# A fused sigmoid attention and ReGLU kernel: first keys in two pieces, values lagging four passes, and three blocks transposed by DMA from ScalarE's queue instead of by TensorE

## Chip, cores, metric

One core of one Trainium2 chip. The metric is the device time in microseconds (us), median of several executions. The span of a trace, from the first to the last instruction, is about 2 us shorter than the time of the same execution.

## The reference

```python
# q, k, v: (8, 12, 448, 64)   w_gate, w_val: (768, 1536)   w_out: (1536, 768), float32
attn = sigmoid(q @ k.T / sqrt(64) - log(448)) @ v            # per batch and head, no softmax
x    = attn.transpose(0, 2, 1, 3).reshape(8 * 448, 12 * 64)
out  = (maximum(x @ w_gate, 0) * (x @ w_val)) @ w_out        # (3584, 768)
```

## The kernel before

The 12 heads of each of the 8 batches are worked in three *blocks* of four heads, 24 blocks in all, numbered 0 to 23; blocks 0 to 2 are batch 0, blocks 3 to 5 are batch 1. A block takes 7 *passes*: in each, `scores` multiplies one 64-wide chunk of keys with all queries and ScalarE takes the sigmoid; `values` multiplies the result with v. Batch 0's attention runs alone; after that the passes of the next batch are put between the feed-forward matmuls of the batch at hand, two or three at a time (a *visit*).

The scores' matmuls read q and k transposed, with the 64 features of a head on the partitions. Before, blocks 0 to 5 are transposed by TensorE, 14 small matmuls for each, and copied out of PSUM by VectorE (a part of block 0's by ScalarE). Blocks 6 to 23 are transposed by the DMA engines, on SP's queue.

```python
def dma_transposes(n):                      # blocks 6 to 23
    for nm in ("k", "q"):
        h16 = qk16.pop((nm, n))
        t2 = qkTp.tile([P, NCH, 2, KC], FP16, tag="qkT", name=f"{nm}T")
        nc.sync.dma_start_transpose(
            t2[:].rearrange("p c h k -> p c (h k)"), h16[:].rearrange("p c r d -> p (c r d)"))
        qkT[nm, n] = t2

def transposes(n, nm, *engines):            # blocks 0 to 5
    ...
    for c in range(NCH):
        nc.tensor.transpose(tr[:, c], h16[:, c, :, :], ident[:])
    ...                                     # copies PSUM -> SBUF

def feed(i):                                # after each pass i of batches 1 to 7
    n, c = divmod(i, NCH)
    ...
    m = n + 1
    if c == 4 and NPRO <= m < NB:           # NPRO = 6
        dma_transposes(m)
    if c == 5 and NBLK < m < NPRO:          # blocks 4 and 5
        transposes(m, "k"); transposes(m, "q")

order = halves("g", 0) + halves("u", 0) + [3] + halves("g", 1) + halves("u", 1)
order += [4] + halves("g", 2) + halves("u", 2) + halves("o", 0) + [5]
order += halves("o", 1) + halves("o", 2)    # weight pieces, and the inputs of blocks 3, 4, 5
...
for b in range(B):
    ...
    for step, cost in enumerate(ffn(b)):
        if b == 0 and step == 12:
            transposes(NBLK, "k"); transposes(NBLK, "q")        # block 3
        if order and step % 8 == 0:
            start_next()                    # load and cast the next of `order`
        if todo and t >= todo[0]:
            todo.pop(0); visit()
```

All weights (18 pieces of 768 KB) are loaded by SP, in one queue, and so are the block inputs but for three of the first (k and v of block 0, k of block 2, on ScalarE's queue). Staging buffers (`sw`, five of them, and `st`, ten) hold what has landed until GpSimd has cast it to fp16.

## Time and profile before

| | |
|---|---|
| time | 434.59 us, median of 3 (434.58 to 435.0) |
| TensorE busy | 97% of the span |
| first feed-forward matmul | 28.25 us |
| DMA engines | full from 2 to 66 us, 380 to 390 GB/s |
| last piece of w_out usable | 67.4 us, 2.7 us before TensorE needs it |

The kernel is a stream of matmuls without gaps once the first attention phase is over, and up to 66 us the DMA engines are just as full. The lines behind this table are in the prediction.

The profiled execution of the kernel before is one of 437.15 us with a span of 434.6: the granted clock of TensorE (the share of its full clock that the profile shows) was 0.50 from 27.8 to 31.2 us. Most other executions have spans of 432.4 to 433.1 at a mean clock of 0.995 to 1.000.

### The profile page before, as it was taken

The numbers are of one execution on the slowest core, as the hardware profiler recorded it, in microseconds if no ns is written. First come the engines' busy times: TensorE is split into PE (matmuls) and PEld (weight loads), VectorE is DVE, ScalarE is ACT, GpSimd is POOL, SyncE is SP. The second block draws the span as 40 slices with busy tenths as digits, with TensorE's granted clock in tenths as the row PEclk, the third lists the DMA queues.
The fourth block names the chain that finished last, engine by engine and source line by source line (L and its number), as shares of the span: only waits on it lengthen the run. The fifth ranks groups of instructions, "written<-read, shape, count | busy, mean of one in ns | idle before, by whom it ended". The sixth has DMA issues, their size and how long they took to land.

```text
span 434.6 us, 7877 instructions
## 1 busy us (share of the span) xinstructions
PE 421.6 (97%) x3292; PEld 216.9 (50%) x3292; DVE 102.8 (24%) x172; ACT 235.6 (54%) x325; POOL 100.6 (23%) x130
## 2 busy tenths in 40 slices
PE   7779999999999999999999999999999999999996
PEld 5334554544455445544455454554455444455553
DVE  3632331123201322113211232023220232212210
ACT  5955656655566555555546556565555556532221
POOL 0287758213301313113031133023130100000000
PEclk9989999999999999999999999999999999999999
DMA  8999999791228910596216932199114320030014
GB/s 306 385 384 386 391 391 271 221 265 72 42 74 231 301 37 16 144 262 170 42 38 193 255 128 44 42 242 293 21 24 109 80 44 2 14 96 1 2 36 110
DMA packets 64100, 66.98 MB, mean 154 GB/s; under 512 B 35776, under 2 KB 54336, under 8 KB 64064
## 3 DMA queue, kind: packets, MB, share of 16 engines
q1 hardware_dynamic: 63088, 64.89, 51.2%
q10 hardware_dynamic: 976, 1.57, 1.0%
q8 instruction: 26, 0.43, 0.4%
q14 instruction: 10, 0.08, 0.1%
HBM read 47.19 MB, written 11.01 MB: 134 GB/s over the span
## 4 chain that ended last, share of the span: by engine, by line
PE 95%; ACT 4%; issue 1%; POOL 0%; DVE 0%; ACTq 0%; POOLq 0%
PE gv_ps L225 51%; PE y_ps L251 26%; PE qk_ps L172 9%; PE pv_ps L196 7%; ACT PT L182 3%; PE tr L157 1%; PE fill L336 1%; ACT gate_sb L237 0%; ACT kT L162 0%; POOL ident masks.py:199 0%; DVE ysb L269 0%; ACT ysb L268 0%; POOL ident masks.py:197 0%; POOL bias_t L63 0%; ACTq L182 0%
## 5 line engine op out<-in xcount | busy, mean ns | idle before, releaser
L182 ACT ACTIVATE PT<-qk_ps,bias_t 128x896 f16<-128x896 f32 x168 | 158.1, 1006 | 55.9 <-PE qk_ps L172 55.7
L225 PE MATMUL gv_ps<-xT,wg 128*128 128x448 f16 x576 | 128.5, 355 | 0.0
L225 PE MATMUL gv_ps<-xT,wv 128*128 128x448 f16 x576 | 128.3, 354 | 0.0
L251 PE MATMUL y_ps<-wo,hT 128*128 128x512 f16 (+1 forms) x672 | 114.1, 326 | 0.0
L237 ACT ACTIVATE gate_sb<-gv_ps 128x448 f32<-128x448 f32 x96 | 52.3, 544 | 93.5 <-PE gv_ps L225 93.5
L240 DVE TENSOR_TENSOR hT<-gate_sb,gv_ps 128x448 f16<-128x448 f32 x96 | 59.6, 621 | 168.7 <-PE gv_ps L225 135.8
L251 PEld LDWEIGHTS <-hT 128*128 128x128 f16 x672 | 64.0, 98 | 48.1 <-issue 7.5
L225 PEld LDWEIGHTS <-wv 128*128 128x128 f16 x576 | 54.8, 98 | 57.1 <-issue 9.1
L225 PEld LDWEIGHTS <-wg 128*128 128x128 f16 x576 | 55.0, 98 | 54.6 <-issue 7.1
L209 DVE TENSOR_SCALAR xT<-pv_ps 128x448 f16<-128x448 f32 x48 | 27.7, 620 | 133.1 <-PE pv_ps L196 133.0
L172 PE MATMUL qk_ps<-qT,kT 64*64 64x448 f16 x672 | 51.6, 360 | 6.6 <-ACT PT L182 6.0
L116 POOL CAST v<-st_v 128x448 f16<-128x448 f32 x21 | 11.8, 562 | 173.2 <-PE pv_ps L196 172.6
L273 ACT ACTIVATE ysb<-y_ps 128x512 f32<-128x512 f32 (+1 forms) x55 | 27.1, 493 | 40.6 <-PE y_ps L251 40.3
L196 PE MATMUL pv_ps<-PT,v 64*64 64x448 f16 x672 | 40.2, 351 | 1.3 <-ACT PT L182 0.8
L172 PEld LDWEIGHTS <-kT 64*64 64x64 f16 x672 | 15.8, 105 | 37.3 <-issue 33.0
L109 POOL CAST h16q<-st_q 128x896 f16<-128x896 f32 x21 | 19.6, 932 | 33.3 <-DMA kT<-h16k 32.5
L196 PEld LDWEIGHTS <-v 64*64 64x64 f16 x672 | 20.1, 107 | 13.5 <-issue 1.8
L109 POOL CAST h16k<-st_k 128x896 f16<-128x896 f32 x21 | 19.6, 932 | 1.3 <-DMA qT<-h16q 0.8
L141 POOL CAST wg<-st_wg 128x1536 f16<-128x1536 f32 x6 | 8.9, 1484 | 18.1 <-DMA st_wg<-in_moe_w_gate_dram 18.1
L117 POOL CAST v<-st_v 64x448 f16<-64x448 f32 x21 | 11.7, 559 | 1.3
L118 POOL CAST v<-st_v 64x448 f16<-64x448 f32 x21 | 11.7, 557 | 0.9
L141 POOL CAST wo<-st_wo 128x1536 f16<-128x1536 f32 x6 | 8.8, 1468 | 6.2 <-DMA st_wo<-in_moe_w_out_dram 6.2
(28 smaller groups left out, 51.6 us busy)
## 6 DMA issues: line engine op xcount, KB each, us to landing
st_q<-in_q_dram SPq DMA_DIRECT2D x24, 448.0 KB, 4.7
out_dram<-ysb SPq DMA_DIRECT2D x54, 192.0 KB, 2.7
st_v<-in_v_dram SPq DMA_DIRECT2D x23, 448.0 KB, 5.9
st_k<-in_k_dram SPq DMA_DIRECT2D x22, 448.0 KB, 5.2
st_wg<-in_moe_w_gate_dram SPq DMA_DIRECT2D x6, 768.0 KB, 11.9
st_wu<-in_moe_w_val_dram SPq DMA_DIRECT2D x6, 768.0 KB, 12.2
st_wo<-in_moe_w_out_dram SPq DMA_DIRECT2D x6, 768.0 KB, 11.9
st_k<-in_k_dram ACTq DMA_DIRECT2D x2, 448.0 KB, 6.6
```

What stands on the lines that cost most here:

```text
L109: eng.tensor_copy(o, i)
L116: eng.tensor_copy(t[:, 0], st[:, 0])
L141: eng.tensor_copy(dst, st[:])
L172: nc.tensor.matmul(ps[o : o + 64, bank, 0:S], kT[r : r + 64, c, h, :], qT[r : r + 64, :, h, :], start=True, stop=True, tile_position=(r, o ...
L182: nc.scalar.activation(pt[:], ps[:, :, 0:S], AF.Sigmoid, bias=bias_t[:], scale=qk_scale)
L196: nc.tensor.matmul(pv[pr][o : o + 64, 0:S], t[r : r + 64, pr, c * D : (c + 1) * D], pt[r : r + 64, pr, :], start=(c == 0), stop=(c == NCH ...
L209: nc.vector.tensor_scalar(out=x[:], in0=pv[pr][:, 0:S], scalar1=XSCALE, scalar2=None, op0=AOP.mult)
L225: nc.tensor.matmul(acc[:, 0:S], w[:, dc, jj * P : (jj + 1) * P], xT[b, dc][:], start=(dc == 0), stop=(dc == NDC - 1),)
L237: nc.scalar.activation(g_sb[:], acc[:, 0:S], AF.Relu)
L240: nc.vector.tensor_tensor(out=hT[f][:, o : o + S], in0=g_sb[:], in1=ps[1][:, 0:S], op=AOP.mult)
L251: nc.tensor.matmul(y[:, 0:mn], hT[f][:, o : o + P], wo[f // FG][:, f % FG, m0 : m0 + mn], start=(f == 0), stop=(f == NFC - 1),)
L273: nc.scalar.activation(ysb[:, m0 : m0 + mn], y[:, 0:mn], AF.Copy, scale=OUT_SCALE)
```

## The change

Three things are meant. The start is to be earlier: K of block 0 comes in two pieces, the fillers (matmuls that nobody reads, issued while the first loads are under way) are wider, v is cast by GpSimd, and values lag four passes instead of two. TensorE is to be relieved of the transposes of blocks 3, 4 and 5, which go to DMA; since SP's queue is full of weights, they are issued from ScalarE's queue, and block 6's pair with them, one visit later than before. Batch 0 gets 11 visits instead of 10. And the last output block is copied out of two PSUM banks side by side. The core of the diff:

```diff
-        load_block(0, ("q", q, nc.sync), ("k", k, nc.scalar), ("v", v, nc.scalar))
+        load_block(0, ("q", q, 0, NCH, sp), ("k", k, 0, 4, act), ("k2", k, 4, NCH, sp), ("v", v, 0, NCH, act))
 ...
-            nc.sync.dma_start_transpose(
+            (nc.scalar if n <= NPRO else nc.sync).dma_start_transpose(
 ...
-        if c == 4 and NPRO <= m < NB:
+        if c >= (5 if m <= NPRO else 4) and m not in transposed and NBLK < m < NB:
+            transposed.add(m)
             dma_transposes(m)
-        if c == 5 and NBLK < m < NPRO:
-            transposes(m, "k")
-            transposes(m, "q")
 ...
-        i1 = min(i0 + (3 if c == 0 else 2), NPASS)
+        i1 = min(i0 + (3 if c == 0 and n > NBLK else 2), i0 + NCH - c, NPASS)
 ...
-            if i >= LAG:                                    # LAG = 2
-                m, cm = divmod(i - LAG, NCH)
-                values(m, [cm])
+            while done <= i - (4 if i < NP0 - 4 else 2):
+                values(done // NCH, [done % NCH])
+                done += 1
 ...
-                count = 3 * NBLK + (1 if b == 0 else 0)
-                lo = 4.0 if b == 0 else 0.0
+                count = 3 * NBLK + (2 if b == 0 else 0)
+                lo = 6.0 if b == 0 else 0.0
 ...
-                if b == 0 and step == 12:
-                    transposes(NBLK, "k")
-                    transposes(NBLK, "q")
+                if b == 0 and step == 4:
+                    dma_transposes(NBLK)
```

More of the change, by code (lines that the diff above doesn't have):

```diff
@@ L86, in load_block, with cast_qk @@
         b, i = divmod(n, NBLK)
-        for nm, src, eng in which:
+        for nm, src, c0, c1, eng in which:
             st = stp.tile([P, 2, S], FP32, tag="st", name=f"st_{nm}")
-            eng.dma_start(
-                st[:],
-                src[b, i * HB : (i + 1) * HB].rearrange("(r h) (p c) d -> (h p) r (c d)", h=2, c=NCH),
-            )
+            rows = src[b, i * HB : (i + 1) * HB].rearrange("(r h) (p c) d -> (h p) r (c d)", h=2, c=NCH)
+            eng.dma_start(st[:, :, c0 * D : c1 * D], rows[:, :, c0 * D : c1 * D])
             staged[nm, n] = st
     def load_all(n: int):
-        load_block(n, ("q", q, nc.sync), ("k", k, nc.sync), ("v", v, nc.sync))
-    def cast_qk(n: int, nm: str, *engines):
+        load_block(n, ("k", k, 0, NCH, nc.sync), ("q", q, 0, NCH, nc.sync), ("v", v, 0, NCH, nc.sync))
+    def cast_qk(n: int, nm: str, *engines, cut=(0, NCH)):
         st = staged.pop((nm, n))
         h16 = h16p.tile([P, NCH, 2, D], FP16, tag="h16", name=f"h16{nm}")
-        cut = [0, 4, NCH] if len(engines) == 2 else [0, NCH]
         for c0, c1, eng in zip(cut, cut[1:], engines):
@@ L151, in dma_transposes, with transposes @@
             qkT[nm, n] = t2
-    def transposes(n: int, nm: str, *engines):
+    def transposes(n: int, nm: str, *engines, cut=(0, NCH)):
         h16 = qk16.pop((nm, n))
         tr = wkp.tile([P, NCH, 2, KC], FP16, tag="wk", name="tr")
-        for c in range(NCH):
+        for c in range(cut[0], cut[-1]):
             nc.tensor.transpose(tr[:, c], h16[:, c, :, :], ident[:])
-        t2 = qkTp.tile([P, NCH, 2, KC], FP16, tag="qkT", name=f"{nm}T")
-        cut = [0, 2, NCH] if len(engines) == 2 else [0, NCH]
+        t2 = qkT.get((nm, n)) or qkTp.tile([P, NCH, 2, KC], FP16, tag="qkT", name=f"{nm}T")
         for c0, c1, eng in zip(cut, cut[1:], engines or (nc.vector,)):
@@ L247, in down @@
         ysb = ysbp.tile([P, DM], FP32, tag="ysb", name="ysb")
+        last = col0 + P == B * S
         for m0, mn in ((0, 512), (512, DM - 512)):
-            y = wkp.tile([P, 512], FP32, tag="wk", name="y_ps")
+            nb = 2 if last and m0 else 1
+            w = mn // nb
+            ys = [wkp.tile([P, 512], FP32, tag="wk", name="y_ps") for _ in range(nb)]
             for f in range(NFC):
-                nc.tensor.matmul(
-                    y[:, 0:mn],
-                    hT[f][:, o : o + P],
-                    wo[f // FG][:, f % FG, m0 : m0 + mn],
-                    start=(f == 0),
-                    stop=(f == NFC - 1),
-                )
+                for j, y in enumerate(ys):
+                    c0 = m0 + j * w
+                    nc.tensor.matmul(
+                        y[:, 0:w],
+                        hT[f][:, o : o + P],
+                        wo[f // FG][:, f % FG, c0 : c0 + w],
+                        start=(f == 0),
+                        stop=(f == NFC - 1),
+                    )
                 if f < NFC - 1:
                     yield mn / 2400.0 + 0.002
-            rows = []
-            for half in range(2):
-                b, r = divmod(col0 + 64 * half, S)
-                o_rows = out[b * S : (b + 1) * S].rearrange("(p c) m -> c p m", c=NCH)
-                rows.append(o_rows[r // KC])
-            last = col0 + P == B * S
-            if last and m0 + mn == DM:
-                h = m0 + mn // 2
-                nc.scalar.activation(ysb[:, m0:h], y[:, 0 : mn // 2], AF.Copy, scale=OUT_SCALE)
-                nc.vector.tensor_scalar(
-                    out=ysb[:, h:DM], in0=y[:, mn // 2 : mn], scalar1=OUT_SCALE, scalar2=None, op0=AOP.mult
-                )
-            else:
-                nc.scalar.activation(ysb[:, m0 : m0 + mn], y[:, 0:mn], AF.Copy, scale=OUT_SCALE)
+            for j, y in enumerate(ys):
+                dst = ysb[:, m0 + j * w : m0 + (j + 1) * w]
+                if j == 0:
+                    nc.scalar.activation(dst, y[:, 0:w], AF.Copy, scale=OUT_SCALE)
+                else:
+                    nc.vector.tensor_scalar(out=dst, in0=y[:, 0:w], scalar1=OUT_SCALE, scalar2=None, op0=AOP.mult)
             if last or m0 + mn == DM:
@@ L276, in down @@
                 for half, eng in enumerate((nc.sync, nc.scalar if last else nc.sync)):
-                    eng.dma_start(rows[half][:, s0 : m0 + mn], ysb[64 * half : 64 * half + 64, s0 : m0 + mn])
+                    b, r = divmod(col0 + 64 * half, S)
+                    rows = out[b * S : (b + 1) * S].rearrange("(p c) m -> c p m", c=NCH)
+                    eng.dma_start(rows[r // KC][:, s0 : m0 + mn], ysb[64 * half : 64 * half + 64, s0 : m0 + mn])
             yield mn / 2400.0 + 0.002
@@ L300, in cast_block @@
         cast_v(n, nc.gpsimd)
+    transposed: set = set()
     def feed(i: int):
@@ L331, in visit, with filler, new_fill @@
         state["pass"] = i1
-    def filler(count: int):
-        t = wkp.tile([P, 512], FP32, tag="wk", name="fill")
-        for _ in range(count):
-            nc.tensor.matmul(t[:, 0:P], ident[:], ident[:], start=True, stop=True)
+    zeros = const.tile([P, 512], FP16, name="zeros")
+    nc.vector.memset(zeros[:], 0.0)
+    fill: list = []
+    def filler(*widths):
+        for w in widths:
+            nc.tensor.matmul(fill[-1][:, 0:w], zeros[:, 0:P], zeros[:, 0:w], start=True, stop=True)
+    def new_fill():
+        fill.append(wkp.tile([P, 512], FP32, tag="wk", name="fill"))
     with tc.manual_schedule():
         nc.scalar.activation(warm[:], bias_t[:], AF.Sigmoid)
-        load_block(0, ("q", q, nc.sync), ("k", k, nc.scalar), ("v", v, nc.scalar))
-        load_block(1, ("q", q, nc.sync), ("k", k, nc.sync), ("v", v, nc.sync))
-        load_block(2, ("k", k, nc.scalar), ("q", q, nc.sync), ("v", v, nc.sync))
+        sp, act = nc.sync, nc.scalar
+        load_block(0, ("q", q, 0, NCH, sp), ("k", k, 0, 4, act), ("k2", k, 4, NCH, sp), ("v", v, 0, NCH, act))
+        load_block(1, ("k", k, 0, NCH, sp), ("q", q, 0, NCH, act), ("v", v, 0, NCH, sp))
+        load_block(2, ("k", k, 0, NCH, act), ("q", q, 0, NCH, sp), ("v", v, 0, NCH, sp))
         def halves(kind, j):
@@ L357, in start_next @@
                 cast_w(*what, nc.gpsimd)
-        filler(40)
-        cast_qk(0, "q", nc.vector, nc.scalar)
-        cast_qk(0, "k", nc.vector, nc.scalar)
+        new_fill()
+        filler(*[512] * 10)
+        cast_qk(0, "q", nc.vector, nc.scalar, cut=(0, 4, NCH))
+        cast_qk(0, "k", nc.vector, nc.scalar, cut=(0, 2, 4))
+        transposes(0, "q")
+        filler(128, 128)
+        transposes(0, "k", nc.scalar, nc.vector, cut=(0, 2, 4))
+        new_fill()
+        filler(128, 128, 128)
+        cast_qk(0, "k2", nc.vector, cut=(4, NCH))
+        for n in range(NBLK):
+            cast_v(n, nc.gpsimd)
         for _ in range(4):
             start_next()
-        transposes(0, "q", nc.vector)
-        transposes(0, "k", nc.scalar, nc.vector)
-        cast_v(0, nc.vector)
-        LAG = 2
-        for i in range(NBLK * NCH + LAG):
+        NP0 = NBLK * NCH
+        done = 0
+        for i in range(NP0 + 2):
             n, c = divmod(i, NCH)
@@ L373 @@
                 scores(n, c)
-            if i >= LAG:
-                m, cm = divmod(i - LAG, NCH)
-                values(m, [cm])
+            while done <= i - (4 if i < NP0 - 4 else 2):
+                values(done // NCH, [done % NCH])
+                done += 1
+            if i == 2:
+                qk16["k", 0] = qk16.pop(("k2", 0))
+                transposes(0, "k", nc.vector, cut=(4, NCH))
+            if 1 <= i <= 3:
+                filler(256)
             if c == 1 and n + 1 < NBLK:
@@ L379 @@
                 cast_qk(n + 1, "q", nc.vector)
-            if c == 4 and n + 1 < NBLK:
-                transposes(n + 1, "k")
-                transposes(n + 1, "q")
-                cast_v(n + 1, nc.vector)
-            if i % 2 == 1 and i < NBLK * NCH:
+            if c in (3, 5) and n + 1 < NBLK:
+                transposes(n + 1, "k" if c == 3 else "q")
+            if 13 <= i < NP0:
                 start_next()
```

## The prediction

> **What bounds the kernel now.** I read the page's engine shares and slices first, then the chain that ended last, then the order of time around the joint between the first attention phase and the first feed-forward phase, and then the DMA by stretches.
>
> The page: TensorE is busy 97% of the span, and only the first slices are below 9. In the DMA row the first six slices (11 us each) are full.
>
> ```profile
> PE   7779999999999999999999999999999999999996
> DMA  8999999791228910596216932199114320030014
> GB/s 306 385 384 386 391 391 271 221 265 72 42 74 231 301 37 16 144 262 170 42 38 193 255 128 44 42 242 293 21 24 109 80 44 2 14 96 1 2 36 110
> ```
>
> The chain in order of time shows who sets the end: fillers and transposes until 7.4 us, then ScalarE's sigmoids (L182), and from 28.3 us TensorE alone.
>
> ```profile
> 1.39 4.45 PE fill L336 x40
> 5.84 1.51 PE tr L157 x14
> 8.23 2.81 ACT PT L182 x3
> 12.91 4.61 ACT PT L182 x5
> 28.32 3.99 PE gv_ps L225 x13
> 61.10 0.89 PE tr L157 x14
> 68.09 3.03 PE y_ps L251 x16
> ```
>
> The 21 sigmoids of batch 0 run from 8.23 to 27.67 us, 0.93 us each; where they run undisturbed they start every 0.90 us. Then 403 us of TensorE follow with no wait. In them three blocks of batch 1 are transposed on TensorE, at 32.3, 46.6 and 61.1 us.
>
> What the chain doesn't show is how near a second bound lies. DMA by stretches (engine columns are busy time; the last three are granted clock, mean busy share of the 16 DMA engines, GB/s):
>
> ```profile
> 2.00:28.00 26.00, 19.14 (x247) 11.50 (x244) 14.44 (x25) 20.84 (x26) 8.56 (x8) 1.00 1.04 381
> 28.00:66.00 38.00, 37.02 (x284) 18.43 (x284) 12.53 (x21) 19.48 (x27) 27.02 (x26) 0.96 1.05 388
> 110.00:113.00 3.00, 3.00 (x18) 1.57 (x16) 0.86 (x2) 1.56 (x3) 0.00 (x0) 1.00 0.82 153
> ```
>
> From 2 to 66 us the DMA engines never rest: 381 x 26 + 388 x 38 = 24.6 MB. The weights are 18 pieces of 768 KB (14.2 MB) and the blocks before the last of them seven of 1344 KB (9.6 MB): 23.8 MB, so the last weight piece lands when nearly all of this has passed. GpSimd's timeline says when it is usable:
>
> ```profile
> 62.03 1.47 POOL L141 CAST wo<-st_wo 128x1536 f16<-128x1536 f32 x1 [4.00 <-DMA st_wo<-in_moe_w_out_dram]
> 64.01 1.47 POOL L141 CAST wo<-st_wo 128x1536 f16<-128x1536 f32 x1 [0.52 <-DMA st_wo<-in_moe_w_out_dram]
> 65.96 1.47 POOL L141 CAST wo<-st_wo 128x1536 f16<-128x1536 f32 x1 [0.48 <-DMA st_wo<-in_moe_w_out_dram]
> 67.92 3.19 PE L251 MATMUL y_ps<-wo,hT 128*128 128x512 f16 x16
> ```
>
> The last w_out piece is ready at 65.96 + 1.47 = 67.4 us. The down projection starts at 67.9 and needs that piece at its eleventh matmul, 10 x 0.216 us later, at 70.1. The slack between TensorE and the weights is **2.7 us**. A gain ahead of this point larger than 2.7 us can't be kept, whatever makes it.
>
> [...] at the start, with both queues in use, it moves no more than the 381 GB/s it moves with one. [...] in the quiet stretch 110 to 113 us only one block's pair moves, 153 x 3 = 459 KB, for 0.82 x 3 = 2.5 us of all 16 engines, 187 GB/s. [...] after the thin end of batch 0 the granted clock is 0.50 from 28 to 31 us, and six 448-column matmuls take 2.42 us there, against 1.16 at full clock. [...] Before, the last two copies share a bank and go one after the other (0.28 us from 430.89, 0.29 from 431.20).
>
> **Part by part.**
>
> *Start.* K is asked for in pieces of 256 and 192 KB, and scores wait for the first only. But q lands at 4.45 us and is still needed whole. Ten 512-column fillers at the cold rate (40 of 128 columns took 4.45 us, so the same time) end near 5.5; then 7 + 2 + 4 narrow matmuls at 0.108 us (14 in 1.51) end near 6.9; ScalarE's copy of 0.37 and the first scores, 0.4, give a first sigmoid at about 7.2 to 7.7 instead of 8.23. With 21 x 0.90 = 18.9 us against the 19.44 taken, up to 0.5 more is possible: values four passes behind, and v casts moved from VectorE to GpSimd (until 17.45 idle), take away what delays a sigmoid. Sum: feed-forward starts 0.5 to 1.5, I take **1.0 us** earlier. The thin end is unchanged (values catch up in passes 17 to 22), so I expect the half-clock window again.
>
> *Transposes of blocks 3, 4, 5.* Three stretches of 0.8 to 0.9 us leave TensorE: **2.6 us**. Added: three pairs of DMA transposes in the full stretch. For 90.5 to 99.75 us, where a pair mixes with full plain traffic, the trace gives 356 GB/s x 9.25 = 3.29 MB; without the pair's 0.46 MB the rest needs 2.83 / 0.388 = 7.3 us, so a pair costs 1.95 us. With 2.5 in the quiet stretch: **2.0 to 2.5 us of DMA each**. Pairs 3 and 4 go ahead of the last weights for certain (their scores come before the down projection), pair 5 probably (its issue falls near 60 us). The order of weights in SP's queue is otherwise the same up to the last piece.
>
> *Visits.* 11 instead of 10, starting later; by the eleventh down matmul both orders have done 17 passes and two values, so the remaining work is the same. One more switch costs about 0.15 us.
>
> *ScalarE.* A transpose's issue takes 1.2 to 1.3 us of its sequencer, 2.5 per block, four blocks. Four PSUM buffers (3.5 us of gate and value matmuls) cover this nearly. But transposes of blocks 5 and 6 are now asked for only one visit ahead (about 3.5 us), in ScalarE's order; issue at +0.6, the second at +1.9, landing 3.0 later is +4.9. Each can hold TensorE for about **1.3 us**; block 5's falls into the wait for weights, block 6's does not.
>
> *Tail.* The last 256 columns in two banks: 24 matmuls of 128 columns (0.064) instead of 12 of 256 (0.11): +0.2; copies side by side: -0.3. Net -0.1.
>
> **Sum.** TensorE alone: 434.6 - 1.0 - 2.6 - 0.1 = 430.9. The weights: ready at 67.4 + 2 x 2.0 = 71.4 at least, 67.4 + 3 x 2.5 = 74.9 at most. Work after the eleventh down matmul is 434.6 - 70.1 = 364.5. So 435.9 to 439.4; with block 6's 1.3 and up to 1.7 for a clock that falls to half while TensorE starves near 63 to 73 us: 437 to 442, in the middle 439.
>
> **Rivals.** (a) The weights don't bind: transposes overlap the plain traffic for nothing, or take little of it. For it: 28:66 reads 1.05, above one, so engines do overlap packets. Against it: the pair's 1.95 us in mixed traffic. It would give 431 to 432 (2.7 us is all that the slack allows). (b) The weights are later by the transposes: 436 to 440, my main reading. (c) The two queues alternate packet by packet; small transpose packets then wait behind 2 KB weight packets, a pair takes 10 us or more to land, and blocks 3 to 5 hold TensorE at their first visits as well. For it: at the start q and k from two queues land 0.75 us apart, as if shared evenly. It adds some 3 us: 441 to 444. (d) ScalarE becomes the bound through its longer queue: with 54% busy and 10 us added it is not, except for moments.
>
> **Range and chances.** I weigh (a) a quarter at 431.5, (b) six tenths at 438.5, (c) the rest at 442: 437. A change of this kind is usually kept because it gained a little, which is why (a) has so much. Range 431.0 to 442.5. Faster by over 2% needs 425.9, below what TensorE alone permits: 0.02. Slower by over 2% needs 443.3, rival (c) at its worst: 0.05. Within 2%: 0.93.
>
> **What would show it.** Right: the first sigmoid between 7.2 and 7.7; feed-forward from about 27.3; no L157 of blocks 3 to 5; casts of w_out ending 4 to 7 us later than 67.4; a wait of TensorE at L251 on GpSimd's L141, near 62 to 74 us; DMA share full until after 70. Wrong: the last w_out cast at 67 to 68 with TensorE not waiting (rival a); or waits of qk_ps on DMA kT or qT of several us before 60 (rival c). A start more than 2 us earlier would break my reading of the first phase.

## The result, and the profile after

**454.44 us**, median of 4 (453.82 to 454.79), against 434.58 for the kernel before in the same rounds: ratio 1.045 (95%: 1.0436 to 1.0473), slower. Here and below a ratio compares the fast runs of one kernel with the other's fast runs of the same rounds, as the record gives it; it is not quite the ratio of the medians quoted. The prediction of 437.0 us with a range to 442.5 was **wrong**.

*The page.* These rows are tenths in 40 slices of 11.3 us, as the prediction shows them for before.

```profile
span 453.0 us, 7794 instructions
...
PE   7765978789999999999999999999999999999996
...
PEclk9997889699999999999999999999999999999999
DMA  8999999269422792159422793059522430021014
GB/s 304 385 364 372 389 232 389 39 162 281 151 42 69 204 267 71 19 162 262 129 42 70 202 254 89 16 156 247 151 42 71 82 70 1 2 69 36 0 36 104
...
PE 80%; DMA 16%; POOL 1%; SPq 1%; issue 0%; ACTq 0%; ACT 0%; DVE 0%; DVEq 0%; POOLq 0%
```

The last line is the chain of work that ended last. Before it was

```profile
PE 95%; ACT 4%; issue 1%; POOL 0%; DVE 0%; ACTq 0%; POOLq 0%
```

TensorE is as full as before from the tenth slice on. What was lost was lost in slices 3 to 9, before 105 us, and there the granted clock is low as well. The chain runs through DMAs for 16% of the span, 72 us, where before it ran through none. That is not what TensorE waited, 16 us (below): these DMAs are loads of weights and inputs as well as transposes. It says that DMA sets the pace there.

*The stretch from 27 to 105 us*, first of before, then of after (busy time of PE, PEld, DVE, ACT and POOL with instructions in brackets, then clock, DMA share, GB/s):

```profile
27.00:105.00 78.00, 76.50 (x606) 38.27 (x602) 20.88 (x35) 43.65 (x59) 44.88 (x49) 0.98 0.96 306
```
```profile
27.00:105.00 78.00, 61.91 (x424) 29.38 (x421) 12.61 (x21) 32.96 (x44) 40.40 (x44) 0.87 0.88 275
```

*What was waited for*, after (engine, line, releaser: us in all, times, longest):

```profile
PE qk_ps L167 <- DMA qT<-h16q: 13.4, 4, 5.0
...
PE gv_ps L220 <- ACT gate_sb L232: 2.5, 1, 2.5
```
```profile
SPq L123 <- DMA kT<-h16k: 9.1, 1, 9.1
SPq L123 <- DMA qT<-h16q: 4.8, 1, 4.8
```

TensorE waited four times for transposed queries, once for each of blocks 3 to 6. It never waited for weights. The second fence is SP's queue: it stood still for 14 us until transposes had landed.

*The order of time* shows the first issues of transposes on ScalarE's queue, and what waited:

```profile
27.97 2.41 ACTq L144 DMA_TRANSPOSE kT<-h16k  x1
...
30.47 3.51 ACTq L144 DMA_TRANSPOSE qT<-h16q  x1
...
34.62 1.68 PE L220 MATMUL gv_ps<-xT,wg 128*128 128x448 f16 x6 [2.52 <-ACT gate_sb L232]
...
43.83 0.96 PE L167 MATMUL qk_ps<-qT,kT 64*64 64x448 f16 x8 [4.34 <-DMA qT<-h16q]
...
54.29 1.24 ACTq L144 DMA_TRANSPOSE kT<-h16k  x1
...
63.29 0.96 PE L167 MATMUL qk_ps<-qT,kT 64*64 64x448 f16 x8 [2.72 <-DMA qT<-h16q]
...
82.07 0.96 PE L167 MATMUL qk_ps<-qT,kT 64*64 64x448 f16 x8 [4.95 <-DMA qT<-h16q]
```

Block 6's scores wait 1.37 us at 98.11. The issues of block 3 held ScalarE's sequencer for 2.41 + 3.51 us. The gate copies stand behind them in ScalarE's order (the first starts at 34.02), the PSUM buffers ran out, and TensorE lost 2.5 us until 34.6. Then block 3's queries, asked for at 30.5, were there at 43.8: 13.3 us, where the DMA transposes of before took a median of 3.4 from issue to landing.

*Why they take so long.* In 39 to 42.5 us, amid block 3's transposes, the DMA view counts packets, and by queue packets, megabytes and share (q1 is SP's queue, with the weights; q10 is ScalarE's, with the transposes):

```profile
DMA packets 1222, 1.36 MB, mean 390 GB/s; under 512 B 630, under 2 KB 647, under 8 KB 1222
...
q1 hardware_dynamic: 611, 1.21, 89.0%
q10 hardware_dynamic: 611, 0.16, 19.7%
```

**611 packets of one queue and 611 of the other.** Here the engines served the two queues in turn, as many packets of one as of the other (whether singly or in equal groups, the counts don't tell). But a transpose's packet had 256 bytes, and a weight's 1.21 MB / 611 = 2.0 KB. So the transposes got an eighth of the bytes. A pair is two tiles of 229,376 bytes, 1792 packets, and so, at the same turns, lets 1792 packets or 3.5 MB of weights pass; (3.5 + 0.46) MB at 390 GB/s are 10.2 us, an estimate from these lines. The pair's packets run from 32.1 to 43.1 us, 11.1 us. For 32 to 43 us the view has 1829 packets of q10 and 1866 of q1, 0.46 MB and 3.43 MB. That is 0.46 MB in 11.1 us, 42 GB/s, where a pair alone had 187 (before, 110 to 113 us). The prediction left this point to a rival.

Turns aren't all of it, and for blocks 4 and 5 they are little. First, a pair starts late while loads are under way. In 28 to 32 us the view has 776 packets of q1 and none of q10; by the packet times of the trace it is 4.1 us from the first issue to the first packet for block 3, 3.6 and 4.1 for blocks 4 and 5, but 1.2 for block 6, which meets no loads. Second, the pair of block 4 ran when the loads had nearly stopped. From 57 to 63 us:

```profile
q10 hardware_dynamic: 1856, 0.46, 93.9%
q1 hardware_dynamic: 286, 0.47, 21.9%
```

That is its whole pair (1792 packets of 256 bytes and 64 of 4). From its first packet at 57.8 to its last at 62.6 only 110 of q1 ran beside it, and beside block 5's (78.2 to 81.5) 219. Even so they took 4.7 and 3.3 us, block 6's alone 2.6. So turns explain the wait at block 3. Those at blocks 4 and 5 come from the late start, the slow run and, at block 5, a short lead: issue at 74.12, TensorE there at 77.1. Why the start is late and the run slow, no run here shows.

*What the waits do to the clock.* The windows at half clock in after (columns as above):

```profile
35.30:38.80 3.50, 3.50 (x12) 1.44 (x10) 0.61 (x2) 0.54 (x1) 1.56 (x2) 0.51 1.08 359
42.20:49.10 6.90, 5.27 (x20) 1.99 (x20) 0.62 (x1) 2.34 (x3) 4.93 (x4) 0.51 1.05 383
62.70:66.10 3.40, 2.81 (x32) 1.68 (x36) 0.00 (x0) 1.91 (x2) 0.00 (x0) 0.50 0.67 226
79.70:86.60 6.90, 4.53 (x42) 2.21 (x43) 0.92 (x2) 2.44 (x3) 2.60 (x4) 0.51 0.33 47
```

At each of the first four waits (the gate, blocks 3, 4 and 5) the clock fell to half (0.50 or 0.51), for 3.4 or 6.8 us. TensorE is busy for 3.50 + 5.27 + 2.81 + 4.53 = 16.1 us in them and by these clocks does half the work: 8.1 us lost, an estimate.

**The account closes.** Waits for transposes 13.4, the wait for a gate 2.5, half clock 8.1; less the half-clock window in before's profiled run (3.40 us busy from 27.8 to 31.2, so 1.7 by the same count), the 2.6 of TensorE's transposes, and 1.2 from the start (first feed-forward matmul at 27.04 instead of 28.25). That is 18.5 us; the spans differ by 453.0 - 434.6 = 18.4. The gate's wait, block 3's and the half clock at both are 2.5 + 4.3 + 4.4 = 11.2 of the 24.0 lost.

*SP's queue.* The program shows why loads wait for transposes of another queue: all its DMAs, of both queues, use eight completion semaphores in turn, and each waits for the one eight places before it in program order. Block 4's kT is the 33rd DMA and a load of w_out the 41st, so that load waits for kT, and SP, which issues in order, with it. SP issued a load at 53.02 us and the next at 62.54, when block 4's kT had landed.

### The profile page after: what moved, and what is told of

Same layout as the page of the kernel before. It is cut to its first block, busy times and chain, and to the rows that moved or that the text cites. A ratio compares the mean times of both kernels' runs of the same rounds, so it can differ in the third digit from the quotient of the medians.

```text
span 453.0 us, 7794 instructions
## 1 busy us (share of the span) xinstructions
PE 425.9 (94%) x3240; PEld 214.5 (47%) x3240; DVE 94.7 (21%) x160; ACT 235.9 (52%) x325; POOL 105.6 (23%) x139
## 4 chain that ended last, share of the span: by engine, by line
PE 80%; DMA 16%; POOL 1%; SPq 1%; issue 0%; ACTq 0%; ACT 0%; DVE 0%; DVEq 0%; POOLq 0%
PE gv_ps L220 43%; PE y_ps L252 24%; PE qk_ps L167 7%; PE pv_ps L191 6%; DMA st_wg<-in_moe_w_gate_dram 5%; DMA st_q<-in_q_dram 2%; DMA qT<-h16q 2%; DMA st_v<-in_v_dram 2%; DMA st_wo<-in_moe_w_out_dram 2%; DMA kT<-h16k 2%; DMA st_k<-in_k_dram 1%; SPq L123 0%; POOL wg L137 0%; SPq L127 0%; ACTq L144 0%
## 5 line engine op out<-in xcount | busy, mean ns | idle before, releaser
L220 PE MATMUL gv_ps<-xT,wv 128*128 128x448 f16 x576 | 130.1, 358 | 0.0
L252 PE MATMUL y_ps<-wo,hT 128*128 128x512 f16 (+2 forms) x684 | 114.6, 324 | 0.0
L220 PEld LDWEIGHTS <-wv 128*128 128x128 f16 x576 | 55.4, 99 | 58.9 <-issue 11.1
L167 PE MATMUL qk_ps<-qT,kT 64*64 64x448 f16 x672 | 52.9, 369 | 18.1 <-DMA qT<-h16q 13.4
L112 POOL CAST v<-st_v 128x448 f16<-128x448 f32 x24 | 13.5, 562 | 183.7 <-PE pv_ps L191 174.5
L264 ACT ACTIVATE ysb<-y_ps 128x512 f32<-128x512 f32 (+2 forms) x56 | 27.4, 489 | 40.7 <-PE y_ps L252 39.4
L191 PE MATMUL pv_ps<-PT,v 64*64 64x448 f16 x672 | 41.5, 366 | 0.8 <-ACT PT L177 0.8
L191 PEld LDWEIGHTS <-v 64*64 64x64 f16 x672 | 21.5, 112 | 13.7 <-issue 4.1
L114 POOL CAST v<-st_v 64x448 f16<-64x448 f32 x24 | 13.7, 570 | 1.0
L113 POOL CAST v<-st_v 64x448 f16<-64x448 f32 x24 | 13.4, 559 | 1.5
L137 POOL CAST wv<-st_wu 128x1536 f16<-128x1536 f32 x6 | 8.8, 1469 | 3.9 <-DMA st_wu<-in_moe_w_val_dram 3.9
```

The costliest lines, as they stand in the source:

```text
L114: eng.tensor_copy(t[64:128, 1], st[0:64, 1])
L137: eng.tensor_copy(dst, st[:])
L167: nc.tensor.matmul(ps[o : o + 64, bank, 0:S], kT[r : r + 64, c, h, :], qT[r : r + 64, :, h, :], start=True, stop=True, tile_position=(r, o ...
L191: nc.tensor.matmul(pv[pr][o : o + 64, 0:S], t[r : r + 64, pr, c * D : (c + 1) * D], pt[r : r + 64, pr, :], start=(c == 0), stop=(c == NCH ...
L220: nc.tensor.matmul(acc[:, 0:S], w[:, dc, jj * P : (jj + 1) * P], xT[b, dc][:], start=(dc == 0), stop=(dc == NDC - 1),)
L252: nc.tensor.matmul(y[:, 0:w], hT[f][:, o : o + P], wo[f // FG][:, f % FG, c0 : c0 + w], start=(f == 0), stop=(f == NFC - 1),)
```

## The experiments

The theory after reading the result: **T**, DMA transposes beside loads take up to four times as long as alone (11.1 and 2.6 us), and TensorE, its clock, ScalarE and SP's queue all wait for that. Rivals: **S**, something in the new start or the visits; **Q**, ScalarE's queue is the fault, not the transposes; **L**, only the lead is too short; **C**, the loss is mostly the clock; **B**, it is the bound set by the weights, as predicted, which hides elsewhere.

### The two halves of the change apart

**e1_tensor**: the changed kernel with blocks 3 to 5 on TensorE again; start, visits and tail stay.

```diff
-            (nc.scalar if n <= NPRO else nc.sync).dma_start_transpose(
+            nc.sync.dma_start_transpose(
 ...
-        if c >= (5 if m <= NPRO else 4) and m not in transposed and NBLK < m < NB:
-            transposed.add(m)
+        if c == 4 and NPRO <= m < NB:
             dma_transposes(m)
+        if c == 5 and NBLK < m < NPRO:
+            transposes(m, "k")
+            transposes(m, "q")
 ...
-                if b == 0 and step == 4:
-                    dma_transposes(NBLK)
+                if b == 0 and step == 12:
+                    transposes(NBLK, "k")
+                    transposes(NBLK, "q")
```

> The changed kernel with blocks 3, 4 and 5 transposed on TensorE again and block 6 from SP's queue; start, visits and tail stay changed. Theory A (the loss is that the DMA transposes of blocks 3 to 6 land late: TensorE waits at their first scores and then runs at half clock): 431.5 to 433.5 us, below the kernel before by the start's 1.2 us and perhaps a half-clock window fewer; no wait of qk_ps on kT or qT. Theory B (the new start, order of loads or visits is at fault): still above 440 us.

435.05 us (433.9 to 435.44), ratio 0.9994 (0.9965 to 1.0022). All of the loss is gone. TensorE's clock is 1.00 and its busy time 77.29 us in the stretch from 27 to 105. But the start's 1.2 to 1.4 us aren't gained either. TensorE now comes to the weights earlier than they are there; its timeline has

```profile
65.81 1.47 POOL L137 CAST wo<-st_wo 128x1536 f16<-128x1536 f32 x1 [0.51 <-DMA st_wo<-in_moe_w_out_dram]
...
67.33 2.33 PE L252 MATMUL y_ps<-wo,hT 128*128 128x512 f16 x16 [0.47 <-POOL wo L137]
```

The last piece of w_out is usable at 67.28 us, as before (67.4), and TensorE, there at 66.86, waits for it. So the bound that the prediction worked out is real, and was met here, without any DMA transpose.

**e2_old_start**: the kernel before with the transposes' part alone (ScalarE's queue, their places, the visits).

```diff
-            nc.sync.dma_start_transpose(
+            (nc.scalar if n <= NPRO else nc.sync).dma_start_transpose(
 ...                                        # feed, visit, count, lo and step 4 as in the change
```

> The kernel before with only the transposes of the change (ScalarE's queue for blocks 3 to 6, their places, the visits). Theory A: the whole loss is here, about 1 us more than the changed kernel, 454 to 457 us. Theory B: 437 us or less.

458.12 us (457.65 to 459.02), ratio 1.0531. The loss is here in full, and somewhat larger: the waits for queries are 14.5 us, the longest 7.3, and those for gates 5.7. With e1, rival S is out.

### How much each block costs

**e3_block3**: e1 with block 3 alone by DMA, from ScalarE's queue at step 4.

```diff
-            nc.sync.dma_start_transpose(                                   # against e1
+            (nc.scalar if n == NBLK else nc.sync).dma_start_transpose(
 ...
-                if b == 0 and step == 12:
-                    transposes(NBLK, "k")
-                    transposes(NBLK, "q")
+                if b == 0 and step == 4:
+                    dma_transposes(NBLK)
```

> The changed kernel with only block 3 by DMA from ScalarE's queue; 4 and 5 on TensorE, 6 from SP. Theory A, from the changed kernel's trace: waits of 4.3 (scores) and 2.5 us (gate copies behind the two issues on ScalarE) plus some 4 us by half clock after them: about 11 us above the run with all on TensorE, 442 to 444 us. Rival C (what costs is the DMA bandwidth that a pair takes from the weights, about 2 us each): at most 3 us above it.

443.45 us (443.02 to 444.29), ratio 1.0196 (1.0163 to 1.0229: whether over 2% is unclear), as expected. One pair costs 8.4 us over e1; the wait at its first scores is 6.2 us.

**e4_blocks456**: the changed kernel with block 3 on TensorE.

```diff
-                if b == 0 and step == 4:
-                    dma_transposes(NBLK)
+                if b == 0 and step == 12:
+                    transposes(NBLK, "k")
+                    transposes(NBLK, "q")
```

> The changed kernel with block 3 on TensorE, blocks 4 to 6 by DMA from ScalarE's queue. Theory A: waits of 3.1, 5.0 and 1.4 us and some 4 us of half clock, less 1.8 us of transposes saved: 441 to 446 us; the losses of this run and of the one with block 3 alone add up to the whole loss within 3 us. Rival C: about 437 us, with TensorE waiting for w_out and not for qT.

450.33 us (449.46 to 450.83), ratio 1.0347: 15.3 us over e1, more than expected. Waits for queries are 11.0 us, the longest 8.2 at block 4. The losses of e3 and e4 add to 8.4 + 15.3 = 23.7, where the whole change loses 454.44 - 435.05 = 19.4. They miss the expected 3 us because a wait at block 3 delays what follows while the loads go on, and later pairs then meet fewer of them: block 4's pair ran beside 1.9 thousand load packets in e4 and took 12.0 us, beside 110 in after and took 4.7.

### Queue, lead, clock

**e7_sp_queue**: the changed kernel with all transposes on SP's queue.

```diff
-            (nc.scalar if n <= NPRO else nc.sync).dma_start_transpose(
+            nc.sync.dma_start_transpose(
```

> The changed kernel with all DMA transposes issued from SP's queue, in the same places of the program. They then stand behind the loads in one queue, and the loads behind their wait for the casts. Theory A says a place behind some 4 MB of loads is 10 us or more as well: TensorE waits at least as long for kT and qT of blocks 3 to 5, while ScalarE's copies of the gate never wait for an issue: 450 to 462 us. If the choice of ScalarE's queue were itself at fault: under 445.

455.63 us (454.64 to 455.73), ratio 1.0466, the same loss. There is no wait for a gate behind an issue any more, and no taking of turns between two queues; instead the transposes stand behind the weights:

```profile
PE qk_ps L167 <- DMA qT<-h16q: 20.8, 2, 11.8
```

So rival Q is out: from either queue the transposes come late behind loads.

**e5_early**: the transposes of block 4 asked for four passes earlier, those of 5 and 6 two.

```diff
-        if c >= (5 if m <= NPRO else 4) and m not in transposed and NBLK < m < NB:
+        if c >= ((1 if m == NBLK + 1 else 3) if m <= NPRO else 4) and m not in transposed and NBLK < m < NB:
```

> The changed kernel, with the DMA transposes of block 4 asked for after the first visit of block 3 and those of blocks 5 and 6 one visit earlier than in the change; block 3 as in the change. Theory A (they land late because each small packet takes turns with a large one of the loads, some 8 to 12 us from issue): with 4 to 12 us more lead the waits at the first scores of blocks 4, 5 and 6 shrink from 3.1 + 5.0 + 1.4 us to under 4 in sum, and most of their half clock goes: 442 to 448 us, near the run with block 3 alone by DMA (443.5). If it is not their lateness but their presence that costs (bandwidth, ScalarE's queue): no faster than 452.

Fast runs 450.2 to 452.09 us, ratio 1.0368 (one slow run of 623.74 at a clock of 0.654 is left out). Better by some 3 us, less than expected. Block 4 no longer waits, but block 3, asked for as in the change, waits 6.0, block 5 waits 5.4, and a new cost appears:

```profile
46.08 5.23 ACTq L144 DMA_TRANSPOSE qT<-h16q  x1
```

In after, block 6's kT, which met no loads, took 1.24 us of ScalarE's sequencer to issue. Here an issue took 5.23, and the gate copy behind it waited 5.2 us (TensorE 1.7 of them). A transpose issued early met more loads: some 1.1 and 1.3 thousand packets beside the pairs of blocks 4 and 5. Rival L holds for a part only.

**e6_warm** and **e6b_warm_again** (the same kernel): idle fillers ahead of the first scores of blocks 3, 4 and 5 keep TensorE busy while it waits.

```diff
         ps = qkp.tile([P, 2, 512], FP32, tag="qk", name="qk_ps")
+        for _ in range({3: 18, 4: 12, 5: 20}.get(n, 0) if c == 0 else 0):
+            nc.tensor.matmul(ps[:, 0, :], zeros[:, 0:P], zeros[:], start=True, stop=True, skip_group_check=True)
```

> The changed kernel with 18, 12 and 20 filler matmuls of 512 columns ahead of the first scores of blocks 3, 4 and 5, as long at full clock (3.9, 2.6, 4.3 us) as TensorE waits there anyway. If the half clock after each wait is a real part of the loss: fewer than 8 us at half clock instead of 20.5, and 447 to 451 us. If the half clock costs nothing (the engine would wait otherwise): 454 to 457.

> The kernel with fillers in the waits once more, for a trace in the fast state. It was no faster (456 to 460) though its mean clock was 0.985 to 0.989 against 0.976. If the chain of loads and transposes sets the pace from 28 to 82 us, and TensorE only waits for it: about 10 us at half clock instead of 20.5, and TensorE arrives earlier at blocks 4 and 5 and waits there longer, with qT landing no earlier than in the changed kernel (43.8, 63.3 and 82 us). If the fillers themselves are late: TensorE has no wait at qT left and fillers end after qT has landed.

e6_warm: 455.95 to 460.32, ratio 1.0534 (one run of 933.0 us is left out; it had a granted clock of 1.000, and TensorE made up 99% of the chain that ended last). e6b: 455.9 and 459.05, ratio 1.0518. The fillers didn't help. In e6b's trace TensorE is at half clock for only 10.2 us instead of 20.5, as expected, but it reaches block 4 no earlier (60.2 us), and block 4's scores start at 70.10 instead of 63.29 us. Their pair was issued 2.8 us earlier (51.45), ran beside 1.6 thousand load packets instead of 110, and took 14.1 us. So the late transposes set the pace and a warmer TensorE only waits for them. Rival C is out as the main cause; in the account it is 8.1 of 24.0 us. What the half clock costs by itself this run can't tell, since block 4's pair changed with it.

### Packets and buffers

**e8_small_rows**: gate and value weights loaded in two column halves, rows of 1 KB instead of 2 KB. If turns go by packets, a pair of transposes must land sooner.

```diff
-            nc.sync.dma_start(
-                st[:].rearrange("p (c f) -> p c f", f=FG * P), src.rearrange("(c p) f -> p c f", p=P)
-            )
+            h = FG * P // 2
+            for f0 in (0, h):
+                nc.sync.dma_start(
+                    st[:].rearrange("p (c f) -> p c f", f=FG * P)[:, :, f0 : f0 + h],
+                    src.rearrange("(c p) f -> p c f", p=P)[:, :, f0 : f0 + h],
+                )
```

> The changed kernel, but gate and value weights are fetched in two column halves, so in rows of 1 KB instead of 2 KB (twice as many loads, same bytes). If a small transpose packet takes turns one for one with a packet of the loads, as the counts of the changed kernel say (611 and 611 in 3.5 us), [...] block 3's pair, 10.9 us of data in the changed kernel, takes 6 to 8.5 us (its first part meets block 4's inputs of 1.8 KB), equal counts in any window of it; the wait of 4.3 us at block 3 shrinks to under 2, and the whole to 446 to 452 us. If the queues shared by bytes or by time: the pair's duration doesn't change, and the time neither.

455.86 us (455.61 to 457.37), ratio 1.0488: no gain. But the turns are seen again, in the DMA view of 33 to 42 us:

```profile
DMA packets 3733, 2.88 MB, mean 320 GB/s; under 512 B 1945, under 2 KB 3733, under 8 KB 3733
...
q1 hardware_dynamic: 1877, 2.42, 86.3%
q10 hardware_dynamic: 1856, 0.46, 27.1%
```

Again as many packets of one queue as of the other, now with 1.3 KB per packet of q1 on average (block inputs are among them), and block 3's pair took 8.9 us of transfer instead of 11.1, not quite the 6 to 8.5 expected. Part of what smaller packets give is lost in the rate, 320 GB/s instead of 354 in the like window. Block 3's scores start at 42.54 instead of 43.83 us. Their wait is no shorter (5.4 us), since TensorE came earlier too. The gain was lost at block 4, whose issue held ScalarE for 5.63 us and TensorE for 2.7.

**e12_swp3**: three weight staging buffers instead of five, so that fewer loads are under way when a transpose comes.

```diff
-    swp = ctx.enter_context(tc.tile_pool(name="swp", bufs=5))
+    swp = ctx.enter_context(tc.tile_pool(name="swp", bufs=3))
```

> The changed kernel with three instead of five staging buffers for weights, so fewer loads stand in SP's queue. Rival D (a transpose must wait for the DMA eight before it, and the DMA eight after it for the transpose; SP then stops loading, 13.9 us in the changed kernel): with fewer loads under way these waits of L123 on kT and qT fall under 4 us and the time to 446 to 451. Theory A alone (packets take turns, as long as any load is under way): no faster than 453, as the loads never stop either way.

452.33 us, ratio of the fast runs 1.0375. Their mean of 451.3 lies between the two expectations, so the time decides nothing. The waits do: from 20 to 110 us no load of SP waits for a transpose any more, and yet TensorE waits longer for queries, 16.5 us instead of 13.4. So the halt of SP's queue isn't the cause of the loss. Block 3's pair now met a gap in the loads (some 150 load packets beside it), took 3.4 us and landed without a wait. Block 4's pair met weights and inputs instead (some 840 load packets, most of them of weights), took 13.3 us, and

```profile
61.86 0.96 PE L167 MATMUL qk_ps<-qT,kT 64*64 64x448 f16 x8 [10.98 <-DMA qT<-h16q]
```

The wait moved on and grew. Turns alone don't explain it: 840 packets are fewer than half of what block 3's pair met in after.

### Is it the loads at all?

**e13_no_weights**: the changed kernel with 17 of the 18 weight loads left out, all weights cast from one piece. **e14_tensor_no_weights** is its twin made from e1. Their outputs are wrong, which doesn't matter for the times.

```diff
+    one_w = wpool.tile([P, WH], FP32, name="one_w")
 ...
-        st = swp.tile([P, WH], FP32, tag="sw", name=f"st_w{kind}")
+        if (kind, j, half) != ("g", 0, 0):
+            staged[kind, j, half] = one_w
+            return
+        st = one_w
```

> Wrong result on purpose: the changed kernel, where only the first weight piece is loaded and every cast reads that piece, so all casts and matmuls stay but 13.4 MB of loads are gone. If the loads of weights are what makes the transposes late: each lands 3 to 5 us after its issue, TensorE waits for them less than 3 us in all, and the time is 429 to 433 us. If ScalarE's queue, the place or the number of the transposes is at fault: still over 442.

> Wrong result on purpose: the same leaving out of 17 weight loads, with blocks 3 to 5 transposed on TensorE as in the first run. 432 to 434.5 us. Beside it the changed kernel without the loads shows what the DMA transposes are worth when DMA is free: if loads are the cause, it is 1 to 3 us faster than this one.

e13: 436.83 us (435.75 to 438.68), ratio 1.0032. e14: 434.4 us (433.29 to 436.6), ratio 0.9982. The difference between DMA and TensorE transposes falls from 19.4 us to 2.4 when the weights' traffic is gone. This is the strongest evidence that the loads make the transposes late: same instructions, same places, same queue. It doesn't part turns, late start and slow run. e13 also missed the expectation that DMA would then win. What is left of the waits in e13:

```profile
35.24 0.57 PE L171 MATMUL qk_ps<-qT,kT 64*64 64x448 f16 x8 [0.30 <-DMA qT<-h16q]
...
52.47 0.96 PE L171 MATMUL qk_ps<-qT,kT 64*64 64x448 f16 x8 [3.00 <-DMA qT<-h16q]
...
68.06 0.57 PE L171 MATMUL qk_ps<-qT,kT 64*64 64x448 f16 x8 [1.48 <-DMA qT<-h16q]
...
81.94 0.57 PE L171 MATMUL qk_ps<-qT,kT 64*64 64x448 f16 x8 [1.38 <-DMA qT<-h16q]
```

Block 4's pair met block inputs, which are still loaded (531 packets of q1 beside it; a wait of 3.0 us and a half-clock window). Blocks 5 and 6 met nothing and still hold TensorE for 1.48 and 1.38 us: that is the short lead of one visit, and the prediction's 1.3 us for it was right. Together 6.2 us of waits are more than the 2.6 us that TensorE saves.

### Is there a version that beats both?

**e9_late_block6**: block 3 on TensorE, blocks 4 and 5 by DMA and early, block 6 on SP's queue, weights asked for twice as often so that they come before block 6's inputs.

```diff
-            (nc.scalar if n <= NPRO else nc.sync).dma_start_transpose(
+            (nc.scalar if n < NPRO else nc.sync).dma_start_transpose(
 ...
-        if c >= (5 if m <= NPRO else 4) and m not in transposed and NBLK < m < NB:
+        if c >= ({4: 1, 5: 3}.get(m, 4)) and m not in transposed and NBLK < m < NB:
 ...
-                if b == 0 and step == 4:
-                    dma_transposes(NBLK)
-                if order and step % 8 == 0:
+                if b == 0 and step == 12:
+                    transposes(NBLK, "k")
+                    transposes(NBLK, "q")
+                if order and step % 4 == 0:
```

> A trial of a version that keeps some of the gain: block 3 on TensorE, only blocks 4 and 5 by DMA from ScalarE's queue (4 asked for at the first visit of block 3, 5 at the second of block 4), block 6 from SP, the last weights ahead of block 6's inputs. Two pairs still take turns with the loads: I expect one of them late by some 3 us, and 437 to 445 us; if lead time is all that was missing, 432 to 434.

448.38 us (447.69 to 448.68), ratio 1.0303, more than expected. Only one wait for queries is left (4.8 us, block 5), but a gate copy waits 6.9 us behind an issue of 5.38 us, and TensorE 4.8 of them.

**e10_tensor_w**: e1 with the weights asked for twice as often.

```diff
-                if order and step % 8 == 0:
+                if order and step % 4 == 0:
```

> All of blocks 3 to 5 on TensorE as in the first run, and the weights asked for every 4 instead of 8 matmuls, so that the last w_out pieces go ahead of block 6's inputs (1.4 MB, about 3.6 us at 385 GB/s). If the start's 1.2 us was lost in the first run because TensorE waited for w_out: 431.5 to 433.5 us and no wait of the down projection. If not: the same 434 to 435 as that run.

434.88 us (434.18 to 435.34), ratio 0.9998 (0.9967 to 1.0028). The last w_out cast ends at 63.84 instead of 67.28 us and TensorE no longer waits for weights, but the time is the same as e1's. In this trace the feed-forward starts at 27.72 us, not 26.89: the start itself varies by 0.8 us from run to run (in e10 scores once wait 1.1 us for kT, in e1 0.4). Its span, 432.0, is 0.4 us or more below the usual ones of before; a gain of that size is within the noise of these rounds. No version tried beats the kernel before.

## Why the prediction was wrong

By its own steps:

- **The start**: the sum is right (feed-forward 1.2 us earlier, 1.0 predicted), its parts are not. The first sigmoid came at 6.84 us, earlier than the 7.2 to 7.7 predicted. The sigmoids then took 19.8 us instead of the 19.44 of before, where 18.9 was hoped for. The two errors cancel: luck.
- **The half-clock window near 28 us**, expected to come again, did not come in after. It did in e3, e4, e5 and e9, which start the same way (e3: from 26.9 us), so it comes and goes. TensorE wasn't idle ahead of the falls traced: in before it was busy for 1.88 of the 3.4 us ahead of 27.8, and in after for 0.7 to 1.3 of the 3.4 us ahead of each fall. How thinly it must be used for one, no run here shows.
- **TensorE saves 2.6 us**: right; no transposing matmul is left in blocks 3 to 5.
- **The tail**: right. The last two copies start 0.12 us apart (449.35 and 449.47) instead of 0.31; from the start of the 512-column copy to the end of the last one it is 1.64 us instead of 1.86.
- **Slack of 2.7 us to the weights**: right for the execution it was read from. In e1 TensorE is at the last piece 3.2 us earlier than before and waits 0.47. But 1.7 us of the slack came from before's half-clock window, so an execution without it has about 1.0 (an estimate). Whether this wait is why the start gains nothing stays open: e10 has none and is no faster, but in its trace the start itself came 0.8 us later.
- **The sum** starts from 434.6, the span of a less lucky execution, and is then read as a time; that the median time was 434.59 is a coincidence.
- **"2.0 to 2.5 us of DMA each"**, and with it the path: this is the step that failed. It took a pair's cost as the bytes it adds to the traffic, which push the weights back, and let TensorE wait for w_out. It carried over the landing of "3.0 later" from a quiet stretch. In its place TensorE waited 13.4 us for qT at the first scores of four blocks, 2.5 behind ScalarE's issues, and never for w_out: from issue to scores block 3's queries took 13.3 us instead of 3. It reached its down projection at 75.66 us, after the weights.
- **The late last cast** (73.22 + 1.47 = 74.7 us, inside the 71.4 to 74.9 worked out) came true by luck. It was to come from full DMA engines. In 57 to 68 us they are counted as busy (share 1.02) but moved only 228 GB/s, after SP had stood still for block 4's transposes. Against 390 GB/s that is 1.8 MB or 4.6 us missed (an estimate from the page), most of the 7.3 us by which the cast is late.
- **Rival (c)** had the mechanism for block 3 almost word for word: queues alternate packet by packet, a pair takes 10 us or more. It also had blocks 3 to 5 hold TensorE at their first visits. It got 15 of 100 chances and the size of "some 3 us", where the change lost about 20. Missing from it or too small were the waits (13.4 us at four blocks), the half clock at them (8.1), and the gate copies behind ScalarE's issue (2.5, sized in the prediction as 1.2 to 1.3 us per issue, measured up to 3.51 in after and 5.63 in variants).
- **Rival (d)**, ScalarE "except for moments": right in that it isn't the bound, but its moments cost 2.5 us in after and up to 5.7 in the variants (e2).
- **One visit's lead costs 1.3 us**: right for block 6 (1.37) and, without weights, for blocks 5 and 6 (1.48 and 1.38).

Shown: that all of the loss comes with the DMA transposes (e1, e2), that most of it needs the weights' traffic (e13, e14), that the queues shared by packets while both had work (611 and 611 in after, 1877 and 1856 in e8), that ScalarE's queue (e7), the half clock (e6b) and SP's halt (e12) are not the main cause. Not shown: how the 20 us divide among late start, turns, slow run and lead, since the waits form a chain and each variant only moved them (e5, e8, e12). The account that closes is one of TensorE's time, not of causes.

Open: in some stretches transposes that began beside loads run on slowly after the loads have stopped. In after, the DMA engines are counted as fully busy there, yet move little (columns as above):

```profile
60.00:62.00 2.00, 0.57 (x3) 0.10 (x1) 0.16 (x1) 0.54 (x1) 0.00 (x0) 1.00 1.44 94
95.00:97.50 2.50, 1.73 (x9) 0.59 (x6) 0.00 (x0) 1.30 (x3) 0.65 (x1) 1.00 0.94 178
```

The second line is a pair alone from its start: 178 GB/s. The first is a pair that began among loads and has none beside it any more: 94. No run here explains the difference.

## What to carry to other kernels

A DMA that is small in bytes wasn't small in time here while another queue was full. With work in both queues, the time of block 3's pair was that of its own bytes plus as many of the *other* queue's packets, at the full 390 GB/s: 10.2 us worked out, 11.1 measured, where block 6's pair took 2.6 alone, and 4.1 us from issue to first packet came on top. Work that out before moving a latency-critical transfer into a stretch where loads fill the engines, and see what lead it has there; beside block 3's pair over seven times its bytes had to pass. And before freeing the engine that bounds a kernel, ask whether what replaces its work is on time; 2.6 us of steady TensorE work were cheaper than 16 us of waits and the half clock at them.
